# Filling rows by plain transfers, constants on another queue and an earlier third group in a retention and mixture-of-experts kernel

## The chip, the cores and the metric

The kernel runs on one core of a Trainium2 chip. The core has five engines with a program each: TensorE (PE in the profile, with its weight loads as PEld), VectorE (DVE), ScalarE (ACT), GpSimd (POOL) and SyncE (SP), which does nothing here but issue transfers and load registers. Engines wait for each other by semaphores; 16 DMA engines carry the transfers. The metric is the device time of one execution in microseconds (us). The kernel before took 424.58 us, the median of 3 runs (424.53 to 425.65).

## The reference

Two steps: a retention layer (a linear attention with a decay for each head) and a mixture of experts that sends every token to one expert.

```python
# q, k, v: 4 batches, 8 heads, 768 positions, 64 features; float32
for t in range(S):
    state = gamma[None, :, None, None] * state + np.einsum('bhd,bhe->bhde', k[:, :, t], v[:, :, t])
    y[:, :, t] = scale * np.einsum('bhd,bhde->bhe', q[:, :, t], state)
x = y.transpose(0, 2, 1, 3).reshape(3072, 512)
logits = x @ w_gate                       # 512 x 8
expert_idx = np.argmax(logits, axis=1)
...
gate_w = probs[np.arange(N), expert_idx]  # softmax of the logits
for e in range(8):
    mask = expert_idx == e
    h = np.maximum(x[mask] @ w1[e], 0.0)  # 512 x 1024
    out[mask] = gate_w[mask, None] * (h @ w2[e])  # 1024 x 512
```

## The kernel before

**Retention.** The 4 x 768 positions are 24 chunks of 128 (NCH; six chunks, CPB, make a batch). A loop over g = 0 to 23 does one chunk in each pass, under an order written out by hand. `load(g)` (L225) brings the 1 MB with q, k and v of a chunk. `scale` (L240, GpSimd) makes vs, v times a power of the decay. `scores` (L251, TensorE, then L254, VectorE) makes the masked products Sb. `update` (L266) adds k times vs to the state U, which ScalarE copies to ub (L269). `carry` (L280) and `output` (L290) sum Y from state and scores, and VectorE multiplies it with the decay table G into xT (L296). `rows` (L307) turns two chunks' xT into token rows, which ScalarE copies to xrow (L308).

**Routing.** Each pair of chunks gets `logits` (L327), whose copy LT is turned by `finish_logits` (L340) into lg. The chunks make groups of 6, 6, 6, 4 and 2 (GROUPS). Of each group, `gating` picks experts on VectorE (`choose`), computes the softmax (`soft`), counts places with small products on TensorE (`rank`, L384 to L388), and turns them into slots (`slots`, `advance`), weights (`weights`) and two more columns of the rows (`label`). Then GpSimd scatters the rows, one indirect transfer for each chunk (`send_rows`, through `scatter_rows`, L663), into the DRAM tensor x_sorted. It has nine regions (E9) of 3072 + 128 rows each: expert 0's first half of the chunks is class 0, expert 0's second half is class 8 (E), and experts 1 to 7 are the others. Behind the last row of every region 128 filling rows are written, also by an indirect transfer (`send_pad`), whose row numbers stand in pads. `declare_no_dep` tells the scheduler that these writes don't overlap, so that they don't wait for one another; reads of x_sorted wait for all writes ahead of them in the program.

For the first three groups the loop has tables by chunk number: finish_at, chosen, ranked, weighed and sends say in which pass each step runs (group i, ending before chunk a + w, is chosen in pass a + w + 1, ranked one pass later, labelled two later, and scattered two chunks at a time in three passes from there).

**Experts.** Weights come as 1 MB parts raw (`fetch`, L129). ScalarE cuts each to a rounded part whi (L137), and VectorE, or GpSimd for class 0, takes the rest wlo (L138); rows are cut alike (L673 turns them, L682 cuts), and each product is three matmuls. fetches and splits are the tables of the passes in which class 0's weight parts 2, 3 are loaded and all four are cut.

Class 0's first 256 rows (xg0, xt0, xhl) are used while the routing of the last groups goes on: `early_half`, with hidden products (L705) and results (L722, yo L726) placed by `fill` and `result` between the rest. Class 8's 256 rows (xg1, xt1, xhl1) are the first item of the main loop, `moe_main`, and experts 1 to 7 follow, the fullest first; their rows come to buf, their hidden products stand at L838 and their results at L863. The order of the experts is found on VectorE (eid7), and SyncE loads each number into a register (L591, `value_load`) before it can address the expert's weights and rows. buf is also G, the decay table, while the retention runs.

**What sets the order.** Each engine runs its own list in program order. SyncE issues every plain transfer, so all loads stand in one list, and the transfers that it issues are queued in that order; a wait of one holds all behind it. GpSimd issues the indirect transfers between its own arithmetic.

Of the kernel before, what the change touches and what calls it, by code (L numbers as in the profile page):

```python
# [20 lines left out]
P = 128  # L21
# [78 lines left out]
def retention_moe(ctx, tc, qkv, wg, w1, w2, cst, gdec, ustr, out):  # L100
# [100 lines left out]
    with ExitStack() as actx:  # L201
# [229 lines left out]
        nc.sync.dma_start(out=cs[:, 0:NFIRST], in_=cst[:, 0:NFIRST])  # L431
        load(0, slice(2, 4))
        load(1, slice(0, 2))
        nc.sync.dma_start(out=G[:, 0], in_=gdec)
        load(1, slice(2, 4))
        nc.sync.dma_start(out=cs[:, NFIRST:], in_=cst[:, NFIRST:])
# [14 lines left out]
        nc.sync.dma_start(out=wgs[:, :, 0:E], in_=wg.rearrange("(k p) e -> p k e", p=P))  # L451
        nc.sync.dma_start(out=us32, in_=ustr)
        for g in range(3, FIRST):
            load(g)
            if g in (7, 10):
# [8 lines left out]
        finish_at = {**{g + 1: t for g, t in quick.items()}, **{2 * t + 4: t for t in slow}}  # L464
        chosen = {a + w + 1: i for i, (a, w) in enumerate(GROUPS[:3])}
        ranked = {a + w + 2: i for i, (a, w) in enumerate(GROUPS[:3])}
        weighed = {a + w + 3: i for i, (a, w) in enumerate(GROUPS[:3])}
        sends = {a + w + 3 + n: (a + 2 * n, a + 2 * n + 2) for a, w in GROUPS[:3] for n in range(3)}
        fetches = {7: 2, 12: 3}
        splits = {g: ((part, 2 * i), (part, 2 * i + 1))  # L470
                  for part, gs in enumerate(((6, 7), (8, 11), (12, 13), (14, 18))) for i, g in enumerate(gs)}
        stages = {}
        last = NCH - 1
        for g in range(NCH):
# [14 lines left out]
            if g in ranked:  # L489
                stages[ranked[g]]["rank"]()  # L490
# [15 lines left out]
            if g == last:  # L506
                token_mask(0, cnt[:, 0:1], EARLY)
                token_index(0)
                hidden, low, result, send = early_half(tc, ld.tile([P, 2, DM], F32, name="yo0", tag="ld"),
# [5 lines left out]
            if g == last - 1:  # L515
                finish_logits(NCH // 2 - 2)
# [11 lines left out]
            if g in ranked:  # L528
                s = stages[ranked[g]]
                s["slots"]()  # L530
                s["advance"]()
                if g == NCH // 2 + 2:
                    s["counts"]()
            if g == 18:
                xg0 = rawp.tile([P, NJ0, SLICE], F32, name="xg0", tag="raw")
                xt0 = rawp.tile([P, KD, EARLY], F32, name="xt0", tag="raw")
            if g == 19:
# [7 lines left out]
            if g == 18:  # L545
# [44 lines left out]
        for i in range(E1):  # L590
            expert_at[i + 1] = nc.sync.value_load(eid7[0:1, i:i + 1], min_val=1, max_val=E - 1)  # L591
# [5 lines left out]
        send_pad(1, xrows[3][:, 0])  # L597
        fetch(1, 0)
        fetch(1, 1)
        xg1 = ld.tile([P, NJ0, SLICE], F32, name="xg1", tag="ld")  # L600
# [405 lines left out]
```

## Time and profile before

| | before |
|---|---|
| median of 3 runs | 424.58 us |
| profiled execution | 423.32 us |
| span of its trace | 421.6 us |
| mean granted TensorE clock | 0.988 |
| DMA traffic | 82.19 MB, mean 195 GB/s over the span |
| scatters of rows (L663, x_sorted<-xrow,KEY) | 24, mean 990 ns |
| scatters of filling rows (L663, x_sorted<-xrow,pads) | 9 |

The span is the time from the first to the last record of one profiled execution; the 1.7 us between it and that execution's own time lie around it. The page gives for each engine the time in which it was busy, then the same in 40 slices of about 10.5 us. In a row of the page or of the timeline stand the start or the group, the busy time, the engine, the line of the kernel, the operation, its tile as output<-input, the shape and the count (x4), and in brackets the idle time ahead of it with what ended it. SPq stands for SyncE's list of transfers. A granted clock of 1.00 is TensorE's full speed.

### The profile page before, as it was taken

The numbers are of one execution on the slowest core, as the hardware profiler recorded it, in microseconds if no ns is written. First come the engines' busy times: TensorE is split into PE (matmuls) and PEld (weight loads), VectorE is DVE, ScalarE is ACT, GpSimd is POOL, SyncE is SP. The second block draws the span as 40 slices with busy tenths as digits, with TensorE's granted clock in tenths as the row PEclk, the third lists the DMA queues.
The fourth block names the chain that finished last, engine by engine and source line by source line (L and its number), as shares of the span: only waits on it lengthen the run. The fifth ranks groups of instructions, "written<-read, shape, count | busy, mean of one in ns | idle before, by whom it ended". The sixth has DMA issues, their size and how long they took to land. (4 is left out here: it accounts for less than half of the span.)

```text
span 421.6 us, 8227 instructions
## 1 busy us (share of the span) xinstructions
PE 399.6 (95%) x3275; PEld 362.0 (86%) x3275; DVE 233.8 (55%) x443; ACT 143.6 (34%) x256; POOL 189.4 (45%) x177
## 2 busy tenths in 40 slices
PE   6899999989798899999999999999999999999994
PEld 3687877778587697999999999999999999999963
DVE  1445646458452546766386557648747665765310
ACT  1033444333341135543154235325415423623100
POOL 1634895885552063100048407605712840850741
PEclk9899999999989999999999999999999999999998
DMA  7999999582436955933645276465664437630111
GB/s 258 410 410 411 416 417 385 182 305 52 153 121 242 211 180 195 287 125 101 152 156 190 85 168 240 138 131 172 241 161 142 152 119 181 236 132 2 49 47 43
DMA packets 42888, 82.19 MB, mean 195 GB/s; under 512 B 5146, under 2 KB 19358, under 8 KB 40032
## 3 DMA queue, kind: packets, MB, share of 16 engines
q1 hardware_dynamic: 37088, 66.56, 48.7%
q0 software_dynamic: 5760, 15.09, 9.6%
q8 instruction: 26, 0.43, 0.4%
q14 instruction: 14, 0.11, 0.1%
HBM read 66.55 MB, written 15.81 MB: 195 GB/s over the span
## 5 line engine op out<-in xcount | busy, mean ns | idle before, releaser
L663 POOL DMA_INDIRECT out<-Z,sidx x80 | 93.5, 1169 | 140.1 <-DVE Z L791 117.6
L138 DVE TENSOR_TENSOR wlo<-raw,whi 128x1024 fp32r<-128x1024 f32 x56 | 67.9, 1216 | 10.2 <-ACT whi L137 9.1
L137 ACT CAST whi<-raw 128x1024 fp32r<-128x1024 f32 (+1 forms) x72 | 67.3, 949 | 8.5 <-DMA raw<-w 8.3
L863 PE MATMUL py<-hh,whi 128*128 128x452 f32 (+5 forms) x192 | 66.9, 349 | 0.0
L863 PE MATMUL py<-hh,wlo 128*128 128x452 f32 (+5 forms) x192 | 66.9, 349 | 0.0
L863 PE MATMUL py<-hl,whi 128*128 128x452 f32 (+5 forms) x192 | 66.9, 348 | 0.0
L843 ACT ACTIVATE hh<-ph 128x256 fp32r<-128x256 f32 (+7 forms) x64 | 31.5, 492 | 99.8 <-PE ph L838 86.0
L844 DVE SCALAR_TENSOR_TENSOR hl<-ph,hh 128x256 fp32r<-128x256 f32 (+7 forms) x64 | 35.5, 556 | 44.9 <-ACT hh L843 37.5
L838 PE MATMUL ph<-xh,whi 128*128 128x452 f32 (+6 forms) x224 | 50.0, 345 | 0.4 <-ACT xh L682 0.4
L838 PE MATMUL ph<-xh,wlo 128*128 128x452 f32 (+6 forms) x224 | 50.2, 346 | 0.0
L838 PE MATMUL ph<-xl,whi 128*128 128x452 f32 (+6 forms) x224 | 50.2, 345 | 0.0
L838 PEld LDWEIGHTS ph<-xh,whi 128*128 128x128 f32 x224 | 40.6, 188 | 1.6 <-ACT xh L682 0.8
L838 PEld LDWEIGHTS ph<-xl,whi 128*128 128x128 f32 x224 | 40.8, 188 | 0.7
L838 PEld LDWEIGHTS ph<-xh,wlo 128*128 128x128 f32 x224 | 40.7, 188 | 0.8
L254 DVE TENSOR_TENSOR Sb<-sp,cs 128x512 f32<-128x512 f32 x48 | 30.8, 683 | 17.6 <-PE sp L251 12.6
L863 PEld LDWEIGHTS py<-hh,wlo 128*128 128x128 f32 x192 | 36.1, 188 | 0.8
L863 PEld LDWEIGHTS py<-hl,whi 128*128 128x128 f32 x192 | 36.1, 188 | 0.8
L863 PEld LDWEIGHTS py<-hh,whi 128*128 128x128 f32 x192 | 36.0, 188 | 0.8
L296 DVE TENSOR_TENSOR xT<-Y,buf 128x512 f32<-128x512 f32 x24 | 16.6, 691 | 35.9 <-PE Y L290 29.9
L682 ACT CAST xh<-buf 128x512 fp32r<-128x512 f32 (+7 forms) x26 | 14.4, 555 | 60.0 <-DVE buf L673 48.9
L786 DVE STREAM_TRANSPOSE Z<-py 128x416 f32<-128x416 f32 (+3 forms) x24 | 15.1, 627 | 26.3 <-PE py L863 24.3
L663 POOL DMA_INDIRECT x_sorted<-xrow,KEY x24 | 23.8, 990 | 12.2 <-issue 5.4
(132 smaller groups left out, 559.4 us busy)
## 6 DMA issues: line engine op xcount, KB each, us to landing
raw<-w SPq DMA_DIRECT2D x32, 1024.0 KB, 14.2
qkv_w<-qkv SPq DMA_DIRECT2D x13, 1024.0 KB, 20.8
qkv_t<-qkv SPq DMA_DIRECT2D x9, 1024.0 KB, 9.3
buf<-x_sorted SPq DMA_DIRECT2D x12, 211.2 KB, 3.8
qkv_t<-qkv SPq DMA_DIRECT2D x4, 512.0 KB
buf<-x_sorted SPq DMA_DIRECT2D x8, 195.0 KB, 3.5
out<-Z,sidx POOLq DMA_INDIRECT x80
xg<-x_sorted SPq DMA_DIRECT2D x8, 130.0 KB
```

The costliest lines, as they stand in the source:

```text
L137: nc.scalar.copy(out=hi[:, h], in_=raw[:, h])
L138: engine.tensor_tensor(out=lo[:, h], in0=raw[:, h], in1=hi[:, h].bitcast(F32), op=ALU.subtract)
L254: nc.vector.tensor_tensor(out=Sb[:, r], in0=sps[r], in1=causal.unsqueeze(1).broadcast_to([P, NP, C]), op=ALU.mult)
L296: nc.vector.tensor_tensor(out=xT.rearrange("a (r m) t -> a r m t", m=2), op=ALU.mult, in0=Y[:, :, 0:2 * C].rearrange("a r (m t) -> a r m t ...
L663: sc = tc.nc.gpsimd.indirect_dma_start(out=dst, out_offset=bass.IndirectOffsetOnAxis(ap=index, axis=0), in_=rows, in_offset=None, bounds_c ...
L682: nc.scalar.copy(out=xh[:, :, sl], in_=src)
L786: nc.vector.transpose(out=Zs[e][:, 0:nb, k, :], in_=py[:, 0:32 * nb].rearrange("p (j c) -> p j c", c=32))
L838: nc.tensor.matmul(out=ph[:, :cap], lhsT=wparts[e, f // 4][a][:, kd, fo:fo + P], rhs=x[:, kd, :cap], start=(n == 0), stop=(n == 3 * KD - 1))
L843: nc.scalar.activation(out=hh[:, :cap], in_=ph[:, :cap], func=AF.Relu)
L844: nc.vector.scalar_tensor_tensor(out=hl[:, :cap], in0=ph[:, :cap], scalar=0.0, in1=hh[:, :cap].bitcast(F32), op0=ALU.max, op1=ALU.subtract)
L863: nc.tensor.matmul(out=py[:, :cap], lhsT=a[:, f % 4, k * P:(k + 1) * P], rhs=x[:, :cap], **se)
```

## The change

Five edits, all in `retention_moe`:

1. The three transfers of constants (cs in two pieces, G's first row) and those of wgs and us32 are issued by ScalarE and no longer by SyncE.
2. Of the first three groups, the third (chunks 12 to 17, ending at SOON = 18) runs every step one pass sooner: lag is 0 for it and 1 for the others. Its last logits are finished in pass 18 behind `output`, and its `rank` stands behind `output` of pass 19.
3. Parts 0, 1 and 3 of class 0's weights are fetched or cut in earlier passes (fetches, splits), and class 0's rows xg0 are loaded in pass 17. yo0 takes a buffer of another pool ("Sb" of wk for "ld").
4. Behind the routing, SyncE loads one expert number only, then issues class 8's rows (xg1 and its meta), then the first weights of expert 1. The other six numbers are loaded behind the rows of expert 1.
5. The filling rows of positions 2 to 7 were six indirect transfers of GpSimd. One stays there and moves ahead; for the five others SyncE loads the row number from pads into a register and writes 128 rows from cs (266 KB) to the region at this row. `disjoint`, taken out of `scatter_rows`, declares them free of dependence on the other writes.

```diff
@@ -428,12 +428,12 @@
             state["half"] += n
 
         load(0, slice(0, 2))
-        nc.sync.dma_start(out=cs[:, 0:NFIRST], in_=cst[:, 0:NFIRST])
+        nc.scalar.dma_start(out=cs[:, 0:NFIRST], in_=cst[:, 0:NFIRST])
         load(0, slice(2, 4))
         load(1, slice(0, 2))
-        nc.sync.dma_start(out=G[:, 0], in_=gdec)
+        nc.scalar.dma_start(out=G[:, 0], in_=gdec)
         load(1, slice(2, 4))
-        nc.sync.dma_start(out=cs[:, NFIRST:], in_=cst[:, NFIRST:])
+        nc.scalar.dma_start(out=cs[:, NFIRST:], in_=cst[:, NFIRST:])
         load(2)
         warm = ps_m.tile([P, 512], F32, name="warm", tag="mt")
 
@@ -448,8 +448,8 @@
         nc.vector.memset(wgs, 0.0)
         nc.vector.memset(exs, 1e-9)
         us32 = ubp.tile([P, P], F32, name="us32")
-        nc.sync.dma_start(out=wgs[:, :, 0:E], in_=wg.rearrange("(k p) e -> p k e", p=P))
-        nc.sync.dma_start(out=us32, in_=ustr)
+        nc.scalar.dma_start(out=wgs[:, :, 0:E], in_=wg.rearrange("(k p) e -> p k e", p=P))
+        nc.scalar.dma_start(out=us32, in_=ustr)
         for g in range(3, FIRST):
             load(g)
             if g in (7, 10):
@@ -461,14 +461,18 @@
         quick = {a + w: (a + w) // 2 - 1 for a, w in GROUPS[:3]}
         slow = [t for t in range(NCH // 2 - 2) if 2 * t + 2 not in quick]
         logits_at = {**quick, **{2 * t + 3: t for t in slow}, NCH - 2: NCH // 2 - 2}
-        finish_at = {**{g + 1: t for g, t in quick.items()}, **{2 * t + 4: t for t in slow}}
-        chosen = {a + w + 1: i for i, (a, w) in enumerate(GROUPS[:3])}
-        ranked = {a + w + 2: i for i, (a, w) in enumerate(GROUPS[:3])}
-        weighed = {a + w + 3: i for i, (a, w) in enumerate(GROUPS[:3])}
-        sends = {a + w + 3 + n: (a + 2 * n, a + 2 * n + 2) for a, w in GROUPS[:3] for n in range(3)}
-        fetches = {7: 2, 12: 3}
+        SOON = NCH - CPB
+        finish_at = {**{g + 1: t for g, t in quick.items() if g != SOON}, **{2 * t + 4: t for t in slow}}
+        finish_last = {SOON: quick[SOON], NCH - 2: NCH // 2 - 2}
+        lag = {a + w: int(a + w != SOON) for a, w in GROUPS[:3]}
+        chosen = {g + lag[g]: i for i, g in enumerate(lag)}
+        ranked = {g + lag[g] + 1: i for i, g in enumerate(lag)}
+        weighed = {g + lag[g] + 2: i for i, g in enumerate(lag)}
+        sends = {g + lag[g] + 2 + n: (GROUPS[i][0] + 2 * n, GROUPS[i][0] + 2 * n + 2)
+                 for i, g in enumerate(lag) for n in range(3)}
+        fetches = {7: 2, 9: 3}
         splits = {g: ((part, 2 * i), (part, 2 * i + 1))
-                  for part, gs in enumerate(((6, 7), (8, 11), (12, 13), (14, 18))) for i, g in enumerate(gs)}
+                  for part, gs in enumerate(((5, 6), (7, 8), (12, 13), (14, 18))) for i, g in enumerate(gs)}
         stages = {}
         last = NCH - 1
         for g in range(NCH):
@@ -486,7 +490,7 @@
             if g % 2 == 0 and g > 0:
                 rows(g - 2)
                 rows(g - 1, tag="mt")
-            if g in ranked:
+            if g in ranked and g != SOON + 1:
                 stages[ranked[g]]["rank"]()
             if g in logits_at:
                 logits(logits_at[g])
@@ -506,14 +510,14 @@
             if g == last:
                 token_mask(0, cnt[:, 0:1], EARLY)
                 token_index(0)
-                hidden, low, result, send = early_half(tc, ld.tile([P, 2, DM], F32, name="yo0", tag="ld"),
+                hidden, low, result, send = early_half(tc, wk.tile([P, 2, DM], F32, name="yo0", tag="Sb"),
                                             wk.tile([P, 4, EARLY], F32, name="rx0", tag="xT"),
                                             wp, ps_m, wparts, xhl, sidxs[0], metas[0], out)
                 fill(FILL[0])
                 carry(g)
             output(g)
-            if g == last - 1:
-                finish_logits(NCH // 2 - 2)
+            if g in finish_last:
+                finish_logits(finish_last[g])
             if g <= LATE:
                 scores(g + 1)
             if g == 2:
@@ -527,14 +531,16 @@
                 s["soft"]()
             if g in ranked:
                 s = stages[ranked[g]]
+                if g == SOON + 1:
+                    s["rank"]()
                 s["slots"]()
                 s["advance"]()
                 if g == NCH // 2 + 2:
                     s["counts"]()
-            if g == 18:
+            if g == 17:
                 xg0 = rawp.tile([P, NJ0, SLICE], F32, name="xg0", tag="raw")
+            if g == 19:
                 xt0 = rawp.tile([P, KD, EARLY], F32, name="xt0", tag="raw")
-            if g == 19:
                 xhl = new_xhl()
             if g < AHEAD:
                 load(FIRST + g)
@@ -542,7 +548,7 @@
                 load(NCH - 5 + g - min(MID.values()))
             elif FIRST <= g < NCH - AHEAD - len(MID):
                 load(g + AHEAD + len(MID))
-            if g == 18:
+            if g == 17:
                 fetch_rows(xg0, 0, NJ0)
                 fetch_meta(metas[0], 0, 2)
             if g in fetches:
@@ -587,22 +593,29 @@
         nc.vector.tensor_tensor(out=se, in0=sel, in1=s7(k_("eid")), op=ALU.mult)
         with nc.allow_low_precision(reason="one nonzero term, a small integer"):
             nc.vector.tensor_reduce(out=eid7, in_=se, axis=AX.X, op=ALU.add)
-        for i in range(E1):
-            expert_at[i + 1] = nc.sync.value_load(eid7[0:1, i:i + 1], min_val=1, max_val=E - 1)
+        place = lambda i: nc.sync.value_load(eid7[0:1, i - 1:i], min_val=1, max_val=E - 1)
         ends = gsm.tile([P, E1], F32, name="ends")
         nc.vector.tensor_tensor(out=ends, in0=cnt[:, 1:E], in1=k_("ebase")[:, 1:E], op=ALU.add)
         nc.vector.tensor_tensor(out=gt, in0=sel, in1=s7(ends), op=ALU.mult)
         nc.vector.tensor_reduce(out=ends, in_=gt, axis=AX.X, op=ALU.add)
         pad_rows(slice(1, E), ends, 0.0)
         send_pad(1, xrows[3][:, 0])
+        xg1 = ld.tile([P, NJ0, SLICE], F32, name="xg1", tag="ld")
+        xt1 = ld.tile([P, KD, EARLY], F32, name="xt1", tag="ld")
+        expert_at[1] = place(1)
+        fetch_rows(xg1, E, NJ0)
+        fetch_meta(metas[E], E, 2)
         fetch(1, 0)
         fetch(1, 1)
-        xg1 = ld.tile([P, NJ0, SLICE], F32, name="xg1", tag="ld")
-        xt1 = ld.tile([P, KD, EARLY], F32, name="xt1", tag="ld")
-        fetch_rows(xg1, E, NJ0)
-        fetch_meta(metas[E], E, 2)
+        send_pad(2, xrows[3][:, 0])
+        for i in range(3, E):
+            row = nc.sync.value_load(pads[0:1, i:i + 1], min_val=0, max_val=E9 * REG - P)
+            sent = nc.sync.dma_start(out=x_rows[bass.ds(row, P)], in_=cs[:, 0:ROW])
+            disjoint(tc, sent, "sorted")
         xg = buf[:, 0:MAXB * SLICE].rearrange("p (j m) -> p j m", m=SLICE)
         fetch_rows(xg, expert_at[1], -(-CAPS[1] // 32))
+        for i in range(2, E):
+            expert_at[i] = place(i)
         fill(2 * KF - state["half"])
         result(0, 0)
         result(0, 1)
@@ -615,8 +628,6 @@
             cut_slices(nc, nc.vector, xhl1[:, 0], xhl1[:, 1], xt1, j, w)
         result(1, 0)
         result(1, 1)
-        for i in range(2, E):
-            send_pad(i, xrows[3][:, 0])
         send(1)
         token_mask(E, cnt[:, E:E9], EARLY)
         token_index(E)
@@ -663,8 +674,12 @@
     sc = tc.nc.gpsimd.indirect_dma_start(
         out=dst, out_offset=bass.IndirectOffsetOnAxis(ap=index, axis=0),
         in_=rows, in_offset=None, bounds_check=dst.shape[0] - 1, oob_is_err=False)
-    tc.declare_no_dep(sc.ins, group=group, reason="every token has one slot: the scattered rows are disjoint")
-    tc.add_to_no_dep_group(group, sc.ins)
+    disjoint(tc, sc, group)
+
+
+def disjoint(tc, transfer, group):
+    tc.declare_no_dep(transfer.ins, group=group, reason="every token has one slot: the rows written are disjoint")
+    tc.add_to_no_dep_group(group, transfer.ins)
 
 
 def turn_slices(nc, xt, xg, j0, w, t0=None):
```

SyncE's list behind the routing, before, from the last of the seven loads of expert numbers (L591) on; raw<-w are expert 1's first weights, xg_1886 are class 8's rows and buf expert 1's:

```order
L591 TENSOR_LOAD eid_98
L591 ISA x2
L129 ISA
L129 DMA raw<-w 128x4x512
L129 ISA
L129 DMA raw<-w 128x4x512
L148 DMA xg_1886<-x_sorted 32x8x130 x4
L152 DMA meta_83<-x_sorted 128x2x2
L148 ISA
L148 DMA buf<-x_sorted 32x15x130
```

And now, from the first load of an expert number on; xg_1819 are class 8's rows, and the four rows from L612 on stand there five times:

```order
L596 TENSOR_LOAD eid_98
L596 ISA x2
L148 DMA xg_1819<-x_sorted 32x8x130 x4
L152 DMA meta_83<-x_sorted 128x2x2
L129 ISA
L129 DMA raw<-w 128x4x512
L129 ISA
L129 DMA raw<-w 128x4x512
L612 TENSOR_LOAD pads
L612 ISA x2
L613 ISA
L613 DMA x_sorted<-cs 128x520
```

Class 8's rows and the weights have changed places, six loads of numbers have gone behind expert 1's rows, and five times a load and a transfer have come in ahead of these rows.

GpSimd's list from the scaling of the last chunks to the first product rows, before; xhl is the cut of class 0's rows, KEY marks a scatter of one chunk's rows, pads one of filling rows, out one of results:

```order
L240 TENSOR_TENSOR vs<-qkv_t,cs 128x512 x2
L401 TENSOR_TENSOR run<-run,tot 128x9
L683 TENSOR_TENSOR xhl<-xt_1341,xhl 128x4x128
L240 TENSOR_TENSOR vs<-qkv_t,cs 128x512
L663 DMA x_sorted<-xrow,KEY 28800x520 x2
L683 TENSOR_TENSOR xhl<-xt_1341,xhl 128x4x128
L663 DMA x_sorted<-xrow,KEY 28800x520 x10
L663 DMA x_sorted<-xrow,pads 28800x520 x2
L663 DMA out<-yo_1639,sidx_88 3072x512
L663 DMA x_sorted<-xrow,pads 28800x520 x6
L663 DMA out<-yo_1639,sidx_88 3072x512
```

And now:

```order
L240 TENSOR_TENSOR vs<-qkv_t,cs 128x512
L401 TENSOR_TENSOR run<-run,tot 128x9
L240 TENSOR_TENSOR vs<-qkv_t,cs 128x512
L674 DMA x_sorted<-xrow,KEY 28800x520 x2
L698 TENSOR_TENSOR xhl<-xt_1419,xhl 128x4x128
L240 TENSOR_TENSOR vs<-qkv_t,cs 128x512
L674 DMA x_sorted<-xrow,KEY 28800x520 x2
L698 TENSOR_TENSOR xhl<-xt_1419,xhl 128x4x128
L674 DMA x_sorted<-xrow,KEY 28800x520 x8
L674 DMA x_sorted<-xrow,pads 28800x520 x3
L674 DMA out<-yo_1639,sidx_88 3072x512 x2
```

Two of the third group's scatters stand ahead of the first cut and two ahead of the second; two, not four, of its six are behind the second cut, in one row with the six of the later groups; and of eight scatters of filling rows three are left.

## The prediction

> **What bounds the kernel now.** I read the page's first line, then the waits of TensorE, then the windows, then the timeline wherever a wait of over a microsecond stood.
>
> ```profile
> PE 399.6 (95%) x3275; PEld 362.0 (86%) x3275; DVE 233.8 (55%) x443; ACT 143.6 (34%) x256; POOL 189.4 (45%) x177
> PE tr L307 <- DVE xT L296: 2.4, 1, 2.4
> PE ph L838 <- ACT xhl L682: 2.1, 1, 2.1
> PE sp L251 <- DMA qkv_t<-qkv: 1.9, 2, 1.5
> PE Y L280 <- ACT ub L269: 0.9, 1, 0.9
> 112.00:114.00 2.00, 0.34 (x4) 0.10 (x1) 0.00 (x0) 0.00 (x0) 0.97 (x1) 1.00 0.61 235
> 114.00:116.00 2.00, 1.23 (x8) 0.91 (x12) 1.56 (x6) 1.28 (x3) 0.00 (x0) 0.70 0.12 46
> 116.00:118.00 2.00, 2.00 (x13) 1.19 (x9) 0.42 (x3) 1.07 (x4) 0.91 (x1) 0.50 0.00 0
> 144.00:400.00 256.00, 255.62 (x1402) 248.04 (x1403) 161.66 (x253) 98.43 (x145) 101.77 (x88) 1.00 0.52 156
> ```
>
> TensorE is the bound (95% busy). A wait row is: who, for what, total, times, longest. A window row is: stretch, length, busy time of PE, PEld, DVE, ACT, POOL, then granted clock, DMA share, GB/s. From 144 to 400 TensorE works 255.62 of 256.00 us, so nothing that the change does to the experts behind the first can pay. All that can be won is ahead of 144: in the waits above and in stretches at half clock (0.50 from 116 to 118).
>
> **Late rows ahead of weights: -2.06 us.** The rows of class 0's second half (xg1, later xhl1) hold TensorE up at the start of the main loop:
>
> ```profile
> 125.20 0.20 DVE L589 TENSOR_REDUCE eid<-se 128x7 int32<-128x49 f32 x1
> L591 SPq TENSOR_LOAD <-eid x7: 3/427/458, 125.4 to 130.1; - x7
> 128.25 0.98 POOL L663 DMA_INDIRECT x_sorted<-xrow,pads  x1 [0.30 <-issue]
> 131.01 1.08 SPq L129 DMA_DIRECT2D raw<-w  x2
> 132.21 2.03 SPq L148 DMA_DIRECT2D xg<-x_sorted  x4
> 134.29 1.08 SPq L152 DMA_DIRECT2D meta<-x_sorted  x1
> 135.57 4.98 SPq L148 DMA_DIRECT2D buf<-x_sorted  x4
> 136.45 0.75 DVE L726 TENSOR_SCALAR yo<-py,meta 128x512 f32<-128x512 f32 x1 [4.25 <-PE py L722]
> 141.83 1.36 DVE L673 STREAM_TRANSPOSE xt<-xg 128x512 f32<-128x512 f32 x3 [4.63 <-DMA xg<-x_sorted]
> 143.92 0.73 PE L838 MATMUL ph<-xhl,whi 128*128 128x256 f32 x4 [2.06 <-ACT xhl L682]
> 148.80 1.04 ACT L137 CAST whi<-raw 128x1024 fp32r<-128x1024 f32 x1
> 95.55 1.81 SPq L148 DMA_DIRECT2D xg<-x_sorted  x4
> 100.51 0.70 DVE L673 STREAM_TRANSPOSE xt<-xg 128x512 f32<-128x512 f32 x1
> ```
>
> SyncE first loads seven expert numbers (125.4 to about 130.8, 0.78 us each), then issues 2 MB of weights, then xg1, which lands 9.6 us after its issue (141.83 against 132.21). The same load of class 0's first half, without weights ahead, was in use 4.96 us after its issue (100.51 against 95.55). In the changed kernel one number is loaded (126.2), then xg1 waits only for the last scatter ahead of it, issued at 128.25. In the kernel before it waited no longer than 132.21, so 132.21 is the latest start, and 137.2 the latest landing. VectorE has yo until 137.2, then the transposes; TensorE's first product stands 2.09 us behind the first transpose (143.92 - 141.83), so the input is ready at 139.3, ahead of TensorE, which ends the work before it at 141.86. The whole wait goes: 2.06. The weights now come 2 us later at most and are cut by ScalarE only from 148.80 on.
>
> **Five filling transfers on SyncE: 0.** What is new on SyncE between the weights and the rows of expert 1 (buf) is five times a register load and a DMA. A load cost 0.78 us, an issue 0.45 to 1.08 (meta's); I take 1.4 for both, 7 us for five. They start when xg1 has landed and the weights are issued (about 137), so buf is issued from 144 plus the landing of the last filling; for a write from this queue no row shows it, the nearest below are 2.8 (meta's landing) and 7.7 (buf's). That is 147 to 152; then 5 us for the four issues at most, and a landing of up to 7.7. The need, and from the list of DMA issues the median us from issue to landing (last number):
>
> ```profile
> 162.33 0.17 DVE L763 SCALAR_TENSOR_TENSOR sidx<-buf,empty 128x15 int32<-128x15 int32 x1
> buf<-x_sorted SPq DMA_DIRECT2D x4, 243.8 KB, 7.7
> meta<-x_sorted SPq DMA_DIRECT2D x2, 2.0 KB, 2.8
> ```
>
> VectorE first uses buf at 162.33; earlier by the 2.06, that is 160.3. With the cheap ends buf lands at about 155, with every dear end at 165; I take the cheap ones, because the queue holds nothing else by then. So 0, with up to +4.5 on the dear end. [...] GpSimd loses the five scatters; they stood behind 144, where TensorE hardly waits for anything.
>
> **Third group sooner: -3.1 us.** The largest wait, 2.43 us, is in the last chunk of the attention:
>
> ```profile
> 94.75 2.03 POOL L240 TENSOR_TENSOR vs<-qkv_t,cs 128x512 f32<-128x512 f32 x2
> 104.38 1.01 POOL L663 DMA_INDIRECT x_sorted<-xrow,KEY  x1 [0.15 <-issue]
> 106.69 1.29 POOL L683 TENSOR_TENSOR xhl<-xt,xhl 128x512 fp32r<-128x512 f32 x1
> 108.29 0.48 PE L705 MATMUL ph<-xhl,whi 128*128 128x256 f32 x2
> 109.78 1.09 PE L290 MATMUL Y<-Sb,vs 128*64 128x128 f32 x16
> 111.74 0.60 PE L307 MATMUL tr<-cs,xT 128*128 128x128 f32 x4
> 112.00 0.97 POOL L663 DMA_INDIRECT x_sorted<-xrow,KEY  x1 [0.30 <-issue]
> 114.02 0.69 DVE L296 TENSOR_TENSOR xT<-Y,buf 128x512 f32<-128x512 f32 x1 [3.01 <-remote]
> 114.77 1.11 PE L307 MATMUL tr<-cs,xT 128*128 128x128 f32 x4 [2.43 <-DVE xT L296]
> 84.47 1.29 DVE L254 TENSOR_TENSOR Sb<-sp,cs 128x512 f32<-128x512 f32 x2 [1.55 <-PE L L327]
> 130.20 0.38 ACT L709 ACTIVATE rx<-ph 128x256 f32<-128x256 f32 x1 [3.17 <-PE ph L705]
> ```
>
> The product Y of chunk 23 ends at 110.87, yet VectorE takes it only at 114.02, though it had nothing else: TensorE's signal came late. It came 1.05 us after GpSimd's last scatter in a row (112.97). The same is seen at 130.20, 0.97 behind the scatter that began at 128.25. I read this as signals of TensorE that are held while GpSimd issues scatters back to back; what holds them no row shows. Behind the wait the clock is low: by the window rows 0.70 of full speed from 114 to 116 and 0.50 from 116 to 118, so 2 x 0.30 + 2 x 0.50 = 1.6 us of TensorE's speed is lost there. The place costs 2.43 + 1.6 = 4.0.
>
> The change issues the six scatters of chunks 12 to 17 one chunk sooner, two of them ahead of each cut of xhl. The first must wait until xg0 has been read, since it writes the same tensor: 100.5 at the latest by the row at 100.51. From there, 1.24 us per scatter (between 1.01 + 0.15 and 0.97 + 0.30), 1.29 per cut, 1.02 for vs: scatters 12, 13 until 103.0; cut until 104.3; vs until 105.3; 14, 15 until 107.8; cut until 109.1; 16, 17 until 111.5 instead of 112.97. The second cut ends at 109.1, not 107.98; TensorE's first product with it stood at 108.29 and the next ones follow at once, so it waits 0.5 to 0.8; I take 0.5. Its work ahead of the last transposes, which ended at 111.74 + 0.60 = 112.34, then ends at 112.85. The signal comes at 111.5 + 1.0 = 112.5, the transposes start 0.75 later, at 113.25: a wait of 0.4. Of 2.43 go 2.43 - 0.5 - 0.4 = 1.5. The clock should hold: it fell behind the wait of 2.43 and, in the rows on the start below, behind one of 1.52, not behind the 0.9 at L280. That gives the 1.6: together 3.1. The ends are 0, if the late signal stays, and 4.0.
>
> On VectorE the choice of this group (seven small operations, 1.4 us) comes one chunk sooner, ahead of Sb of chunk 20; the row of Sb shows that VectorE stood idle for 1.55 us ahead of it, which covers them. If not, they cost TensorE 1.4 at most.
>
> **Constants on ScalarE's queue: 0.**
>
> ```profile
> 5.53 0.43 SPq L225 DMA_DIRECT2D qkv_t<-qkv  x1
> 14.92 1.29 PE L251 MATMUL sp<-qkv_t 64*128 64x128 f32 x16 [1.52 <-DMA qkv_t<-qkv]
> 0.00:15.00 15.00, 9.97 (x110) 5.93 (x111) 3.89 (x10) 2.22 (x4) 4.48 (x9) 1.00 0.86 299
> 16.00:17.00 1.00, 1.00 (x10) 0.86 (x10) 0.82 (x2) 0.00 (x0) 0.90 (x1) 0.50 1.01 410
> ```
>
> TensorE waits at 14.92 for chunk 2, and the clock falls after it. DMA is 0.86 busy up to there, so bytes set that landing, and the change leaves every byte ahead of chunk 2 where it was and puts 80 KB (wgs, us) ahead too. SyncE's issue at 5.53 is not what is late. The ends: 80 KB at 299 GB/s, +0.3; or the 14% of idle DMA time is filled, the wait of 1.52 goes and the low clock behind it with it, at the 1.6 of the other place: -3.1. I take 0, the nearest row being the busy share.
>
> **Fetch and splits of class 0 sooner: 0.** They are off TensorE's path but for one wait of 0.9 us for ub behind ScalarE's cut of a weight that had not landed; that weight keeps its place in the queue of transfers. Bounds -0.9 and 0.
>
> **Sum.** -2.06 - 3.1 = -5.2. The profiled execution took 423.32 us (span 421.6), so a profiled one should take 418.1. The unprofiled runs have a median of 424.58, 1.26 above it; for their median I forecast 424.58 - 5.2 = **419.4**.
>
> **Rivals.**
> - *The late signal stays.* The last two scatters still lie beside Y of chunk 23, since the chain above is only 1.5 us shorter. For it: signals were also late in pairs of scatters (84.47). Then -2.06 alone: 422.5. Chance 0.21.
> - *The start gains too*: -3.1 more, 416.3. For it, the idle 14%; against it, the bytes. 0.12.
> - *The wait shrinks but the half clock stays*, because the fall is set by windows of time and not by this wait: -2.06 - 1.5, 421.0. For it, the 16:17 row, where a wait of 1.52 was enough. 0.08. [...]
> - *The new input of the main loop is late elsewhere* (VectorE held up by yo): the 2.06 stays, -3.1 alone, 421.5. 0.04.
> - *Slower: SyncE's filling transfers hold back buf.* Each waits until the one ahead has landed, and TensorE stands at the first product of expert 1. With 2.8 for a landing (as meta) one costs 1.4 + 2.8 = 4.2, five 21. Of these 160.3 - 7.7 - 5 - 2.8 = 144.8 leaves 144.8 - 137 = 7.8 free, so TensorE stands for 13.2 and the time is 419.4 + 13.2 = 432.6. The gain is used up from (7.8 + 5.2) / 5 = 2.6 us each, and from 2.9 it is slower by what can be told. Against it: earlier scatters lie 1.27 us apart without waiting for landings. 0.04; a disturbed order of the early chunks adds 0.01.
> - The forecast: 0.50.
>
> Eight in ten lie from 416.2 to 422.9, where the first two rivals and the forecast's ends (419.4 + 2.1 if TensorE's waits for the cut and for VectorE stay longer) are taken in. About 0.3% (1.3 us) can be told from no change: faster means under 423.3. All cases but the slower one lie there by their middle; the first, at 422.5, loses a quarter of its chance to the scatter of its unknowns. Faster 0.87, same 0.08, slower 0.05.
>
> **What would show it.** Right: no wait of L838 for xhl; the two scatters ahead of each cut; the last of the six ending near 111.5; L296 of the last chunk within 1.2 us of it and no clock of 0.50 behind; the row 14.92 where it is, within 0.5; buf in use without a wait. Wrong: a wait of L705 for the cut over 1 us; a wait of L863 or L838 behind 144; a new stretch at half clock.

## The result and the profile after

The changed kernel took **413.97 us** (median of 4 runs, 413.62 to 414.14), the kernel before 425.12 beside it (4 runs, 424.53 to 425.96): a ratio of 0.9735, 95% interval 0.9714 to 0.9757. It is 11.15 us faster, where 5.2 were forecast, and it lies below the range of 416.2 to 422.9. The profiled executions took 423.32 and 413.62 us (spans 421.6 and 411.8), 9.7 apart.

TensorE's waits in the changed kernel (for what, total, times, longest), the seven longest:

```profile
PE sp L251 <- DMA qkv_t<-qkv: 2.1, 3, 1.1
PE Y L280 <- DVE xT L296: 1.6, 1, 1.6
PE Y L280 <- ACT ub L269: 1.5, 1, 1.5
PE L L327 <- DVE lg L344: 1.4, 3, 0.7
PE U L266 <- POOL vs L240: 1.1, 1, 1.1
PE warm L442 <- DVE ones L162: 1.1, 1, 1.1
PE L L327 <- DVE rk L394: 0.6, 1, 0.6
```

The waits of 2.43 for xT in the last chunk, of 1.6 at the first result product and of 2.06 for xhl are gone, and nothing stands behind the first product of the main loop. (Lines behind 430 have moved: L705, L722, L838, L861 and L863 are now L720, L737, L853, L876 and L878; L591 is L596, L663 is L674; in the experiments' kernels they stand 0 to 15 lines further down than before, so L840 and L865 of e3 are L838 and L863.) The timeline of the changed kernel at the steps of the forecast:

```profile
13.74 1.16 PE L251 MATMUL sp<-qkv_t 64*128 64x128 f32 x16 [0.86 <-DMA qkv_t<-qkv]
99.13 1.01 POOL L674 DMA_INDIRECT x_sorted<-xrow,KEY  x1 [2.96 <-DMA meta<-x_sorted]
108.96 0.98 POOL L674 DMA_INDIRECT x_sorted<-xrow,KEY  x1 [0.30 <-issue]
110.62 0.69 DVE L296 TENSOR_TENSOR xT<-Y,buf 128x512 f32<-128x512 f32 x1 [0.47 <-PE pf L388]
110.90 1.12 PE L307 MATMUL tr<-cs,xT 128*128 128x128 f32 x8
112.58 0.64 PE L327 MATMUL L<-xT,wgs 128*32 128x256 f32 x8 [0.56 <-DVE rk L394]
117.57 0.18 PE L384 MATMUL pf<-EA,us 128*128 128x18 bf16 x1 [0.37 <-DVE sh L377]
124.78 0.50 PE L737 MATMUL py<-whi,hh 128*128 128x512 f32 x1
126.86 1.79 SPq L148 DMA_DIRECT2D xg<-x_sorted  x4
131.47 1.36 DVE L688 STREAM_TRANSPOSE xt<-xg 128x512 f32<-128x512 f32 x3 [0.17 <-DMA xg<-x_sorted]
135.80 0.64 PE L853 MATMUL ph<-xhl,whi 128*128 128x256 f32 x4
137.02 0.97 POOL L674 DMA_INDIRECT out<-yo,sidx  x1 [1.88 <-DVE m L192]
144.47 1.95 SPq L148 DMA_DIRECT2D buf<-x_sorted  x4
151.74 0.18 DVE L778 SCALAR_TENSOR_TENSOR sidx<-buf,empty 128x15 int32<-128x15 int32 x1 [0.52 <-DMA buf<-x_sorted]
```

And of the kernel before, the rows at the same work which the prediction didn't show:

```profile
115.81 1.08 PE L327 MATMUL L<-xT,wgs 128*32 128x256 f32 x8
121.87 0.18 PE L384 MATMUL pf<-EA,us 128*128 128x18 bf16 x1 [0.36 <-DVE sh L377]
130.64 0.50 PE L722 MATMUL py<-whi,hh 128*128 128x512 f32 x1 [1.59 <-ACT rx L709]
PE py L861 <- ACT hh L843: 0.4, 1, 0.4
PE ph L838 <- ACT xh L682: 0.4, 1, 0.4
PE py L861 <- issue: 0.3, 1, 0.3
```

The lead of the changed kernel at each is the difference of the starts:

| up to | before | after | lead | gained since the row above |
|---|---|---|---|---|
| first transposes behind the loop (L307) | 111.74 | 110.90 | 0.84 | 0.84 |
| last group's products (L384) | 121.87 | 117.57 | 4.30 | 3.46: the wait of 2.43, the low clock behind it, less 0.56 of a new wait for rk |
| first result product (L722, now L737) | 130.64 | 124.78 | 5.86 | 1.56: the wait of 1.59 for rx |
| first product of the main loop (L838, now L853) | 143.92 | 135.80 | 8.12 | 2.26: the wait of 2.06 for xhl |
| end of the span | 421.6 | 411.8 | 9.8 | 1.7: the waits of 0.4, 0.4 and 0.3, and 0.6 in places that the waits don't list |

### The profile page after: what moved, and what is told of

Read it like the earlier page. It is cut to its first block, busy times and chain, and to the rows that moved or that the text cites. A ratio compares the mean times of both kernels' runs of the same rounds, so it can differ in the third digit from the quotient of the medians.

```text
span 411.8 us, 8249 instructions
## 1 busy us (share of the span) xinstructions
PE 395.7 (96%) x3275; PEld 359.8 (87%) x3275; DVE 234.7 (57%) x443; ACT 144.2 (35%) x256; POOL 185.4 (45%) x172
## 5 line engine op out<-in xcount | busy, mean ns | idle before, releaser
L674 POOL DMA_INDIRECT out<-Z,sidx x80 | 93.8, 1172 | 140.8 <-DVE Z L806 118.2
L878 PE MATMUL py<-hh,whi 128*128 128x452 f32 (+5 forms) x192 | 66.9, 349 | 0.0
L878 PE MATMUL py<-hh,wlo 128*128 128x452 f32 (+5 forms) x192 | 66.9, 349 | 0.0
L878 PE MATMUL py<-hl,whi 128*128 128x452 f32 (+5 forms) x192 | 66.9, 348 | 0.0
L853 PE MATMUL ph<-xh,wlo 128*128 128x452 f32 (+6 forms) x224 | 50.2, 346 | 0.0
L853 PE MATMUL ph<-xl,whi 128*128 128x452 f32 (+6 forms) x224 | 50.2, 345 | 0.0
L853 PE MATMUL ph<-xh,whi 128*128 128x452 f32 (+6 forms) x224 | 49.9, 345 | 0.0
L853 PEld LDWEIGHTS ph<-xh,whi 128*128 128x128 f32 x224 | 40.7, 188 | 0.9
L853 PEld LDWEIGHTS ph<-xl,whi 128*128 128x128 f32 x224 | 40.8, 188 | 0.7
L853 PEld LDWEIGHTS ph<-xh,wlo 128*128 128x128 f32 x224 | 40.7, 188 | 0.8
L878 PEld LDWEIGHTS py<-hh,wlo 128*128 128x128 f32 x192 | 36.1, 188 | 0.8
L878 PEld LDWEIGHTS py<-hl,whi 128*128 128x128 f32 x192 | 36.1, 188 | 0.8
L878 PEld LDWEIGHTS py<-hh,whi 128*128 128x128 f32 x192 | 36.0, 188 | 0.8
L674 POOL DMA_INDIRECT x_sorted<-xrow,KEY x24 | 23.8, 992 | 13.6 <-issue 4.8
```

Source lines behind the costliest of these rows:

```text
L674: sc = tc.nc.gpsimd.indirect_dma_start(out=dst, out_offset=bass.IndirectOffsetOnAxis(ap=index, axis=0), in_=rows, in_offset=None, bounds_c ...
L853: nc.tensor.matmul(out=ph[:, :cap], lhsT=wparts[e, f // 4][a][:, kd, fo:fo + P], rhs=x[:, kd, :cap], start=(n == 0), stop=(n == 3 * KD - 1))
L878: nc.tensor.matmul(out=py[:, :cap], lhsT=a[:, f % 4, k * P:(k + 1) * P], rhs=x[:, :cap], **se)
```

## The experiments

Four sets of runs were made, each on a chip of its own, with the kernel before beside the others. There it took 418.63, 418.47, 418.56 and 418.03 us, **not 425.12**. So the first comparison holds something that none of the later ones had; it is looked for below (the record names no chip for the first pair). Each ratio is against the kernel before of the same set.

| run | median us | ratio, 95% interval |
|---|---|---|
| e1 constants alone | 418.87 | 1.0015 (0.9991 to 1.0038) |
| e2 third group alone | 424.16 | 1.0147 (1.0107 to 1.0187) |
| e3 late rows alone | 419.75 | 1.0030 (1.0013 to 1.0048) |
| e4 late rows and filling transfers | 412.39 | 0.9859 (0.9828 to 0.9889) |
| e5 kernel before again | 419.15 (one run) | |
| e6 changed kernel | 412.74 | 0.9868 (0.9836 to 0.9901) |
| e7 late rows, yo0 elsewhere | 420.20 | 1.0042 (1.0017 to 1.0067) |
| e8 late rows, result's scatter first | 413.17 | 0.9883 (0.9846 to 0.9921) |
| e9 changed, old third group | 411.82 | 0.9817 (0.9788 to 0.9846) |
| e10 changed, old constants | 413.15 | 0.9867 (0.9828 to 0.9907) |
| e11 changed, filling by GpSimd | 421.18 | 1.0061 (1.0036 to 1.0085) |
| e12 a pair of scatters behind the loop | 418.72 | 1.0000 (0.9980 to 1.0021) |
| e13 a longer row of scatters | 417.96 | 0.9997 (0.9976 to 1.0017) |

### One part at a time: e1 to e4

e1 takes only the five constants' transfers of the change into the kernel before:

```diff
-        nc.sync.dma_start(out=cs[:, 0:NFIRST], in_=cst[:, 0:NFIRST])
+        nc.scalar.dma_start(out=cs[:, 0:NFIRST], in_=cst[:, 0:NFIRST])
...
```

> The kernel before with the constants on ScalarE's queue alone. Theory A (each edit acts at its own place): chunk 2 arrives about 1.2 us sooner, the clock stays at 1.00 from 10 to 20 us, TensorE is 2.0 us ahead from there on, and the wait of the third group at the last chunk stays: 425.1 - 2.0 = 423.1. Theory B (the lead is eaten by the next wait, since all later waits are set by transfers or GpSimd): within 0.5 us of the kernel before, 424.6 to 425.1.

e2 takes only the tables and the loop of the attention (the earlier third group, fetches, cuts, xg0, and yo0's new place):

```diff
+        SOON = NCH - CPB
...
-        fetches = {7: 2, 12: 3}
+        fetches = {7: 2, 9: 3}
```

> The kernel before with the third group one pass sooner, with the earlier fetches and cuts of class 0 that go with it. Theory A: the wait of L307 for xT (2.43) and the low clock behind it (1.1) go: -3.4, and the wait of L722 for rx (1.6) goes only if the signal there comes in time by chance: 420 to 421.7. Theory B (the signal that came late moves with the scatters): the waits come back in other rows, 424 to 425.

e3 takes only the new order of SyncE's list; the filling rows stay with GpSimd:

```diff
-        fetch(1, 0)
-        fetch(1, 1)
 ...
+        expert_at[1] = place(1)
         fetch_rows(xg1, E, NJ0)
         fetch_meta(metas[E], E, 2)
+        fetch(1, 0)
+        fetch(1, 1)
```

> The kernel before with class 8's rows ahead of the weights and one expert number loaded ahead of them; all filling rows stay with GpSimd. Theory A: the wait of L838 for xhl (2.06) goes and nothing comes in its place: 425.1 - 2.1 = 423.0; with the waits of 0.4, 0.4 and 0.3 in the main loop still there. Theory B (the later weights or the second half's rows hold up what follows): under 1 us won, over 424.1.

e4 is e3 with the filling transfers too:

```diff
+        send_pad(2, xrows[3][:, 0])
+        for i in range(3, E):
+            row = nc.sync.value_load(pads[0:1, i:i + 1], min_val=0, max_val=E9 * REG - P)
+            sent = nc.sync.dma_start(out=x_rows[bass.ds(row, P)], in_=cs[:, 0:ROW])
+            disjoint(tc, sent, "sorted")
...
-        for i in range(2, E):
-            send_pad(i, xrows[3][:, 0])
```

> As the run with the late rows ahead, with the filling rows of five positions as plain transfers of SyncE as well. Theory A: the plain transfers alone change nothing that TensorE waits for, the same time within 0.5 us as without them (423.0). Theory B: GpSimd, freed of five scatters, lets TensorE's signals through sooner, and the small waits of the main loop go: 1 us less than without, 422.0.

The expectations were worked out from 425.1, so they are read as differences. The constants win nothing (Theory B of e1). The third group alone costs 5.5 us, which neither theory had. The late rows alone win nothing and cost 1.1 (Theory B of e3, with a little more), and with the filling transfers, which were to change 1 us at most, the time falls by 7.4. Why e3 wins nothing stands in the timeline of e3 (SyncE, VectorE, GpSimd, ScalarE, TensorE) and in two windows of it:

```profile
126.69 1.79 SPq L148 DMA_DIRECT2D xg<-x_sorted  x4
131.27 1.36 DVE L675 STREAM_TRANSPOSE xt<-xg 128x512 f32<-128x512 f32 x3 [0.43 <-DMA xg<-x_sorted]
145.34 0.97 POOL L665 DMA_INDIRECT x_sorted<-xrow,pads  x1 [13.26 <-DMA buf<-x_sorted]
150.89 1.29 DVE L675 STREAM_TRANSPOSE buf<-buf 128x512 f32<-128x512 f32 x2
153.32 0.97 POOL L665 DMA_INDIRECT out<-yo,sidx  x1 [0.30 <-issue]
158.74 1.14 ACT L684 CAST xh<-buf 128x512 fp32r<-128x512 f32 x2 [9.44 <-issue]
162.74 1.88 PE L840 MATMUL ph<-xh,whi 128*128 128x452 f32 x4 [4.55 <-ACT xh L684]
184.60 0.37 PE L865 MATMUL py<-hh,whi 128*128 128x452 f32 x1
162.00:164.00 2.00, 1.26 (x3) 1.17 (x4) 1.51 (x3) 1.73 (x3) 1.09 (x1) 0.50 0.29 54
164.00:166.00 2.00, 2.00 (x7) 1.74 (x6) 2.00 (x4) 0.59 (x1) 1.31 (x2) 0.50 1.16 209
```

Class 8's rows now come in time (131.27). But expert 1's first cut xh, whose input VectorE had turned by 152.2, starts at 158.74, and TensorE stands for 4.55 us behind it, then works at half clock. GpSimd issues six filling scatters from 145.34 on, which write x_sorted and so wait until expert 1's rows have been read, and only behind them, at 153.32, the second scatter of class 0's results. The row doesn't name what ScalarE waited for; candidates are the filling scatters and that scatter of yo0, whose memory the main loop's tiles take over. The semaphore records of the same trace (the times at which engines and transfers signal) show that it was the second: ahead of the cut ScalarE's list stands from 147.10 to 158.70 at two semaphores, of which one had been reached at 142.32, and the other is that of the scatter of yo0, which lands at 158.67. In e4 that scatter is issued at 135.18, and the cut follows VectorE's transposes:

```profile
150.52 1.21 ACT L691 CAST xh<-buf 128x512 fp32r<-128x512 f32 x2 [2.59 <-DVE buf L682]
```

### Which scatter it was: e5 to e8

e5 is the kernel before, for its trace; e6 the changed one:

> The kernel before once more, for its profile where the four runs above were made (there it took 418.6 us, not 425.1). Theory A (TensorE's signals are on time here, so that it comes earlier to the main loop and waits there for class 8's rows): no wait of L307 for xT, a wait of L838 for xhl of 5 to 6 us. Theory B (the same waits as in the first profile, all shorter): L307 about 1.5, L838 about 2.

> The changed kernel where the others were run. Theory A (late rows and filling transfers carry the gain): within 1.5 us of the run with these two alone (412.4), 411 to 414. Theory B (the third group costs here what it cost alone, 5.5 us): 416 to 418.

e7 changes one tile of e3, as the change does:

```diff
-                hidden, low, result, send = early_half(tc, ld.tile([P, 2, DM], F32, name="yo0", tag="ld"),
+                hidden, low, result, send = early_half(tc, wk.tile([P, 2, DM], F32, name="yo0", tag="Sb"),
```

> As the run with the late rows alone, with yo0 (class 0's results) in the buffer that the changed kernel gives it. Theory A (there ScalarE's cut xh waited for the scatter of these results, since xh takes over their memory, and not for expert 1's rows): the wait of L840 for xh (4.5) goes: 415.2. Theory B (the cut waits for the six scatters of filling rows, or for signals that they hold up): the wait stays, 419.7.

e8 changes one place in the order of e3:

```diff
+        send(1)
         for i in range(2, E):
             send_pad(i, xrows[3][:, 0])
-        send(1)
```

> As the run with the late rows alone, with the second scatter of class 0's results issued ahead of the six scatters of filling rows and not behind them. Theory A (xh waits for this scatter alone): it lands before 141, the wait of 4.5 goes: 415.2. Theory B (xh waits for the filling rows): 419.7.

e8 bears it out: the six filling scatters go out when they did in e3, one scatter of results has moved ahead of them, and 6.6 of the 7.4 us of the filling transfers are there (419.75 - 413.17; the kernel before differs by 0.16 between the two sets). Its rows:

```profile
136.70 0.97 POOL L665 DMA_INDIRECT out<-yo,sidx  x1 [4.47 <-DVE m L192]
152.18 0.97 POOL L665 DMA_INDIRECT x_sorted<-xrow,pads  x1 [0.30 <-issue]
151.77 1.22 ACT L684 CAST xh<-buf 128x512 fp32r<-128x512 f32 x2 [2.31 <-DVE buf L675]
158.18 0.97 PE L840 MATMUL ph<-xh,whi 128*128 128x452 f32 x4
177.85 0.37 PE L865 MATMUL py<-hh,whi 128*128 128x452 f32 x1
```

The cut starts while a filling scatter is still to be issued (152.18), so it doesn't wait for those. The size agrees: e3 loses the wait of 4.55, and from L840 to L865 it needs 184.60 - 162.74 = 21.86 where e8 needs 177.85 - 158.18 = 19.67, so 2.2 more at low clock; together 6.7. The 2.2 were in no theory.

In e7 the wait went to another tile. ScalarE's row names it, and TensorE's wait follows:

```profile
154.71 0.94 ACT L845 ACTIVATE hh<-ph 128x256 fp32r<-128x256 f32 x3 [12.21 <-DMA out<-yo,sidx]
PE py L863 <- ACT hh L845: 5.3, 1, 5.3
```

Whichever tile takes yo0's memory waits for the scatter that reads yo0. So Theory A had the cause right, and its number wrong: the new place is no cure.

The kernel before has, in e5, the other wait in its place:

```profile
108.22 1.09 PE L290 MATMUL Y<-Sb,vs 128*64 128x128 f32 x16
109.37 0.69 DVE L296 TENSOR_TENSOR xT<-Y,buf 128x512 f32<-128x512 f32 x1
109.52 0.97 POOL L663 DMA_INDIRECT x_sorted<-xrow,KEY  x1 [0.30 <-issue]
127.09 1.98 SPq L148 DMA_DIRECT2D xg<-x_sorted  x4
138.90 1.23 PE L838 MATMUL ph<-xhl,whi 128*128 128x256 f32 x4 [3.94 <-ACT xhl L682]
140.00:142.00 2.00, 2.00 (x11) 2.00 (x11) 1.76 (x12) 0.13 (x1) 0.00 (x0) 0.50 0.81 115
```

VectorE takes the last chunk's Y at 109.37, 0.06 behind its end (109.31), although GpSimd is in its row of four scatters there (the third from 109.52). So nothing holds TensorE's signal, it is through with the work ahead of the main loop at 134.96 (138.90 - 3.94) and not at 141.86, and it stands 3.94 us for class 8's rows, again with the clock at 0.50 behind. e3 trades this wait for the one for xh, and only the two cures together pay: e4 and e8.

### One part taken out: e9 to e11

e9 is the changed kernel with the old tables and loop of the attention, e10 with the constants on SyncE (the diffs of e2 and e1 backwards):

> The changed kernel with the third group, the fetches, the cuts and yo0 where they were before. Theory A (where TensorE's signals are on time, the earlier group wins nothing and costs the wait of 1.8 for the second cut): 411 to 412.7, the same or up to 1.8 below the changed kernel (412.7), if the kernel before takes 418 to 419 there. If it takes 425 there (late signals): 416 to 418. Theory B (the earlier group carries a gain of its own everywhere): 414.5 or more.

> The changed kernel with the constants back on SyncE. Theory A (bytes set the arrival of chunk 2, the queue is no matter): 412.7 within 0.8. Theory B (the 2.0 us that the first profile of the changed kernel had gained by chunk 3 come from the queue): 414.7.

e11 gives the filling rows back to GpSimd:

```diff
-        send_pad(2, xrows[3][:, 0])
-        for i in range(3, E):
...
+        for i in range(2, E):
+            send_pad(i, xrows[3][:, 0])
         send(1)
```

> The changed kernel with six filling scatters back on GpSimd, ahead of the second scatter of class 0's results, as before the change. Theory A (what takes over yo0's memory, hh here, waits for that scatter): a wait of TensorE for hh of about 5 us, 417 to 419. Theory B (yo0's new place is enough): 412.7 within 0.8.

Without the filling transfers all of the gain is gone and 2.6 more (421.18), with a wait of the expected kind and size, and half clock behind it; the expectation was 2 to 4 us low since it left the clock out once more:

```profile
PE py L873 <- ACT hh L855: 5.6, 1, 5.6
156.00:158.00 2.00, 1.44 (x3) 1.16 (x4) 1.09 (x3) 1.88 (x5) 0.00 (x0) 0.50 0.00 0
158.00:160.00 2.00, 2.00 (x6) 1.60 (x5) 1.98 (x2) 0.94 (x1) 0.00 (x0) 0.50 0.00 0
```

The constants' queue is worth nothing (413.15 against 412.74 in e6, on another chip, the intervals of the ratios almost the same). The old third group gives 411.82, the lowest median of all; its ratio of 0.9817 against the 0.9868 of e6 speaks for Theory A, but the intervals overlap by a hair (0.9836 to 0.9846). What the earlier group costs stands in the waits of e6 and is missing in those of e9:

```profile
PE ph L720 <- POOL xhl L698: 1.8, 1, 1.8
```

The same wait of 1.8 stands in e2, there with the clock at 0.50 behind it (110 to 112 us), beside one of 1.8 for hh (which waits for the scatter of yo0, from its new place) and one of 0.8 for xh. Together with some 1.6 us of clock behind the first they are about 6 us, an estimate from these waits and the window rows (0.99 from 60 to 110 us, 0.50 from 110 to 112, 0.95 from 112 to 114), where the part alone costs 5.5. The wait of 3.9 for xhl in e2 is no part of this: e5 has it too.

### The late signals: e12 and e13

e12 issues scatters 16 and 17 behind the loop; e13 issues all six of the third group in the last pass:

```diff
-            for i in range(*sends.get(g, (0, 0))):
+            for i in range(*sends.get(g, (0, 0)) if g < last else (0, 0)):
...
+        for g in range(*sends[last]):
+            send_rows(g)
```

> The kernel before with the last two scatters of the third group behind the loop, out of the way of the last chunk's product Y. Theory A (late signals come with a row of scatters): where the kernel before takes 425, the wait of L307 for xT and the low clock behind it go, 421.5; where it takes 418.5, there is nothing to win, within 0.8. Theory B (the wait there has nothing to do with these scatters): no change in either case.

```diff
+        sends = {**{g: r for g, r in sends.items() if r[0] < GROUPS[2][0]}, NCH - 1: (GROUPS[2][0], GROUPS[2][0] + 6)}
```

> The kernel before with all six scatters of the third group behind the second cut, so that they and the next groups' make a longer row of scatters beside the last chunk's product Y. Theory A (a row of scatters by itself holds TensorE's signals): VectorE takes Y a microsecond or more behind its end, a wait of L307 or L327 of 2 to 4 us, low clock behind it, and over 2 us more than the kernel before. Theory B (what held the signals in the first measurement is absent here, whatever the scatters): VectorE takes Y on time, and the time is that of the kernel before within 1 us, less what the later routing costs class 8's rows, at most 2.4.

Neither changes the time. e12 can't tell its theories apart where the kernel before takes 418.5. In e13 VectorE takes Y on time in the middle of six scatters:

```profile
109.02 1.09 PE L290 MATMUL Y<-Sb,vs 128*64 128x128 f32 x16
109.78 0.97 POOL L664 DMA_INDIRECT x_sorted<-xrow,KEY  x1 [0.30 <-issue]
110.26 0.69 DVE L296 TENSOR_TENSOR xT<-Y,buf 128x512 f32<-128x512 f32 x1
```

So a row of scatters did not hold TensorE's signals by itself here: Y ends at 110.11 and is taken 0.15 later. What held them in the first profile, 3.15 us there (110.87 to 114.02), is **not settled**: none of the later traces has the wait of L307 for xT or that of L722 for rx. One more thing sets the first pair apart: its two traces hold 3518 and 3744 semaphore records, the thirteen later ones 4813 to 4840, for much the same number of instructions (8222 to 8250 in all fifteen). So part of the events is missing there; whether that has to do with the late signals, no run shows. It also means that releasers and landing times read from these two traces rest on part of the events.

## Why the prediction was wrong

Two steps failed. The time fell out of the range because places got no term, or 0, that gave 4.1 us of the 9.8 us of span: the wait for rx (1.56), all that stands behind 144 (1.7) and the start (0.84). And the mechanism failed at the five filling transfers, put at 0: without them the late rows gain nothing (e3), with them 7.4 us more come (e4).

**Late rows, -2.06: right in the first pair, wrong about why it was safe.** There the wait went and 2.26 were gained; xg1 was issued at 126.86 and in use at 131.47, both inside the bounds. But the step costed the move by itself, and where it was made by itself it gained nothing (e3). It took the rows of expert 1 for the next need, 160.3; the next need was the memory of yo0. That the 2.06 came out is in part luck: the change moved the scatter of yo0 forward as well, by the edit that the sum put at 0.

**Five filling transfers, 0: the mechanism that failed.** SyncE's side came out on the cheap end or better: the loads and issues of the five took 6.75 us (forecast 7), buf was issued at 144.47 (forecast 147 to 152) and in use at 151.74 (forecast 155). The list of DMA issues of the changed kernel has their landing:

```profile
x_sorted<-cs SPq DMA_DIRECT2D x5, 260.0 KB, 5.2
```

That lies between the ends of 2.8 and 7.7; in the trace of e4 it is 7.8 (6.1 to 7.9), at the dear end, and buf was still not late: e4 has no wait of TensorE for a cut of it. GpSimd's side failed: "they stood behind 144, where TensorE hardly waits for anything". That was read from a kernel in which the wait for xhl came first and covered the next. Behind the six scatters stood the scatter of class 0's results, and behind that the first tile of expert 1. In the first profile this shows on ScalarE's list alone: it stands until 161.53 at the semaphore of that scatter (issued at 156.28), and TensorE came to xh only at 166.88. The term is not 0 but, beside the late rows, -7.4 (e4 against e3), or +8.4 if taken back (e11 against e6).

**Third group, -3.1: near in size in the first pair, empty elsewhere.** There the place gave 3.46, the wait gone and the clock at 1.00. The six scatters ended at 109.94, not at 111.5, since the first of them began at 99.13 and not at 100.5. In the other sets the wait wasn't there in the kernel before, and the part costs a wait of 1.8 for the second cut, which the forecast had put at 0.5. The step's premise, signals held by rows of scatters, does not hold in e5 and e13; what held them in the first pair is open, so its size there is not shown to have come for the reason given. Nor does its rule for the clock (it falls behind a wait of 1.52 and not behind 0.9) come out of the later traces: with waits of 1.57 and 1.84 near the start e4 kept full clock, and behind one of 1.5 e12 did not (0.50 from 16 to 18).

**The wait for rx, 1.6: left out.** It stood in the list of waits and in a row (130.20) that the prediction used for something else. It got no term, and 1.56 came from it.

**Constants, 0: right in time.** e1 and e10 show nothing. One sign was missed: the row at 14.92, which was to stay within 0.5, came to 13.74 in the first pair and to 13.56 in e6, but to 15.29 in e1, where the constants alone are moved, and to 13.65 in e4, where they are not. So whether the queue brings chunk 2 sooner is open; no time came of it. The full clock near 16 us in the first pair is not the queue's doing: a clock of 0.50 also stands in the traces of e6 (18 to 20 us), e11 (16 to 18; both with the constants on ScalarE) and e12 (16 to 18; on SyncE), and those of e9 (ScalarE), e5 and e10 (SyncE) have 1.00 from 14 to 20. The 0.84 that the first pair has by the last chunk is not traced to a cause.

**Behind 144, nothing to win: 1.7 us off,** 1.1 of it in waits of 0.3 to 0.4. The one for hh came from a late signal again: ScalarE takes at 402.82 a product that TensorE had ended at 398.05. The causes of the others were not followed; e5 has none of them.

So the sum of 5.2 met 9.8 of span: 3.46 + 2.26 for its two terms, and 1.56 + 1.7 + 0.84 without one. In the medians 1.4 more came on top: the profiled execution of the kernel before (423.32) lies 1.80 under its median, that of the changed kernel 0.35. Where the signals are on time the change is worth 5.7 us (418.47 - 412.74), near the 5.2, but that is luck, since the reasons are others: a wait of 3.94 and its clock at L838, kept from coming back by the filling transfers. The rival that ended slower looked at the right edit, with the wrong sign.

## What to carry to other kernels

Before a wait is costed as gain, follow the next engine down to the memory: a tile that takes over another's buffer waits for the last reader of that buffer (here TensorE stood 4.55 us for it in e3 and 5.3 in e7), which can be a scatter at the end of a long row on an engine that looks idle. When such a reader stands behind work that waits for something else, moving it one place ahead can be worth as much as rewriting that work: e8 gets 6.6 of 7.4 us by moving one line. And a trace of one execution can hold waits that the same kernel doesn't have elsewhere (2.43 for xT in the first profile, none in e5); terms that rest on a wait without a known cause should be kept apart in the sum. Every wait in the list needs a term, be it 0 with a reason: the 1.6 for rx had none.

## What was not expected of the hardware

The same kernel took 425.1 us in one measurement and 418.0 to 418.6 on four chips later; in the trace the difference lies in TensorE's signals, which in the first one reached VectorE and ScalarE late beside rows of scatters, by 3.15 us at the last chunk and by 4.8 near the end (398.05 to 402.82); at the last chunk VectorE took Y 0.06 us behind its end in e5 and 0.15 in e13.

And a long stop of TensorE cost clock besides in these runs: behind the waits of 5.8 (e1) and 4.55 us (e3) the lost speed comes to 1.4 and 2.3 us, behind those of 3.94 (e5) and 5.6 (e11) to at least 2.5 and 1.7, an estimate from half of TensorE's busy time at 0.50 in the window rows, which in e5 and e11 end while the clock is still low. In e3 a wait of 4.55 cost 6.7 in all, against e8.

How long the wait was did not settle it alone. In the first profile the clock fell behind the waits of 1.52 and 2.43, and behind that of 2.06 (141.86 to 143.92) it stayed at 1.00. Up to the last matmuls the clock records of this trace have two stretches at 0.50, from 15.82 and from 114.81, each 3.41 us long; their starts lie 98.99 us apart, which is 29 times 3.41. In e11 the window rows put two such starts at 14.72 and 154.64, 139.9 apart, which is 41 times 3.41. In the first profile TensorE was idle for 1.75 us of the 3.41 ahead of the first (12.40 to 15.82) and for 2.43 of those ahead of the second (111.39 to 114.80); the stretch from 142.11 to 145.53, eight times 3.41 behind the second start, has 1.81 us idle, and no lower clock came behind it. So in these two traces the falls keep a beat, which speaks for the rival that set them by windows of time; how much idle time it takes, these cases don't settle. And e2 and e6 have the same wait of 1.8 for the second cut, e2 with a clock of 0.50 behind it (110 to 112), e6 with 1.00 from 60 to 120: it cost some 1.6 us more in the one, by the estimate above, and nothing in the other.
